# Masking the score tiles of the first six attention tiles on VectorE, and a new order of three GpSimd steps

## The chip, the cores and the metric

The kernel runs on one core of a Trainium2 chip, as one launch. The metric is the device time of that launch in microseconds (us), the median of several runs. The core's engines work side by side, each through a queue of its own: TensorE (PE in the profile; PEld are its weight loads), VectorE (DVE), ScalarE (ACT), GpSimd (POOL) and SyncE (SP), which here only issues DMA transfers. An engine takes its instructions strictly in the order in which they stand in its queue, and waits where an instruction needs something that another engine has not finished.

## What is computed

Three layers, one after the other, over 3072 tokens of width 384, all in float32. The first is a linear attention with a decaying state, 4 batches by 8 heads, 768 steps, head size 48:

```python
for t in range(S):
    kt, vt, rt, wt = (k[:, :, t], v[:, :, t], r[:, :, t], w[:, :, t])
    cur = np.einsum('bhd,bhe->bhde', u[None] * kt, vt)
    y[:, :, t] = np.einsum('bhd,bhde->bhe', rt, state + cur)
    state = wt[:, :, :, None] * state + np.einsum('bhd,bhe->bhde', kt, vt)
```

The second layer is an MLP, and the third a mixture of 8 experts of which each token takes the best one:

```python
h = x @ w_in;  g = np.maximum(h, 0.0) + alpha * np.minimum(h, 0.0);  x = g @ w_out
...
expert_idx = np.argmax(x @ w_gate, axis=1)
h = np.maximum(xe @ w1[e], 0.0);  ye = h @ w2[e];  out[mask] = gate_w[mask, None] * ye
```

## The kernel before

**Tiles and blocks.** The attention works in 24 tiles of 128 tokens, and three tiles make one of 8 blocks, on which the MLP then works (16 steps f of 128 hidden columns each). The attention of a block's tiles runs between the MLP steps of the block before. Block 0's MLP has a further job in it: `w_in` and `w_out` arrive as float32 and are split into a high and a low part, so that a product of float32 matrices can be made of three faster matmuls. The expert layer follows from about 560 us on.

**One attention tile**, with the names of the trace. `ex` (L291) is the running product of the decays; r is multiplied by it (L306, POOL) and k by its inverse `rec` (L315 to L331; L333, all DVE). PE then makes the scores, keys by queries, for eight heads in two PSUM tiles `pa` (L371). Only keys that lie before the query may count, so ACT copies each `pa` to `at` in SBUF (L379), and POOL sets the rest of `at` to zero (L383). The query's own key is dealt with apart: POOL multiplies r, k and u over the 48 elements of a head (`rk`, two steps, L338 and L339), DVE sums them to one number `c` per head (L344), and POOL multiplies v by it (`cv`, L351, two instructions). The state needs the transposed keys (`kt`, L401, ACT) and the decays over a whole tile (`pm`, L362, ACT), and is updated on DVE or POOL (L423 to L426). PE makes the output from `at`, `cv` and the state (L438 to L459), and DVE and ACT take it out of PSUM in a high and a low part (`xth`, `xtl`, L464, L469).

**MLP steps.** PE makes nine matmuls into `ph` (L611; there are two `ph` buffers), ACT takes the negative part `gn` (L614), DVE adds it to `ph` (`gt`, L616, which frees `ph`), and ACT and DVE split the result (`gh`, L622; `gl`, L624) for the nine matmuls of the second product (L637). When a block's sixteen steps are done, the three PSUM tiles `py` are copied to `x` (L648: the second on DVE, the others on ACT), and PE's next block needs their place. DVE then forms the gate's sums from `x` (L512).

**Weights.** Per piece of weights ACT copies the raw words (L216), DVE takes them apart in three integer steps (L220, L221, L224), ACT casts the high part (`wih`, `woh`, L237), and DVE subtracts to get the low one (`wil`, `wol`, L241).

**What sets the order.** `OPS` gives for each of a tile's steps a slot, counted from the tile's own start slot `s_tile(i)` in units of one MLP step; the prologue (tiles 0 to 2, and the start of tile 3) has a table of its own, `PRO_OPS`. In the prologue all engines run in the order of the slots. From then on PE and POOL do, while a scheduler sets the order of DVE, ACT and SP from its own model of costs; for the last part PE and DVE go by the slots. `constants()` builds small tables on POOL at slot 34, among them `tri`, a 128x128 triangle of ones. `rk` and `cv` have one buffer each, `ps_a`, the PSUM pool of `pa`, has three.

Of the kernel before, what the change touches and what calls it, by code (L numbers as in the profile page):

```python
# [11 lines left out]
BF16 = mybir.dt.bfloat16  # L12
# [3 lines left out]
ALU = mybir.AluOpType  # L16
# [10 lines left out]
NP = H // 2  # L27
# [39 lines left out]

NBACK = 7

DMW = 2 * 512 + NP * 129 + 1  # L70


OPS = {
# [3 lines left out]
}  # L77
# [30 lines left out]
def attention_mlp_moe(ctx, tc, dmaj, tmaj, ub, alpha, w_in, w_out, w_gate, w_gate_b, wexp, out):  # L108
    nc = tc.nc
    vec, act, pool, pe, sp = nc.vector, nc.scalar, nc.gpsimd, nc.tensor, nc.sync  # L110
# [3 lines left out]
    cst = ctx.enter_context(tc.tile_pool(name="cst", bufs=1))  # L114
# [17 lines left out]
    def load_tile(i):  # L132
        if i < NB:
            both = wp.tile([128, DMW + TMW], F32, tag="W", name="both")
            dm, tm = both[:PR, :DMW], both[:, DMW:]
            if i == 0:
# [4 lines left out]
        else:  # L141
            dm = ap.tile([PR, DMW], F32, tag="dm", name="dm")
            tm = ap.tile([128, TMW], F32, tag="tm", name="tm")
# [23 lines left out]
    pool.memset(inj, 0.0)  # L167
    ident = cst.tile([128, 128], F32, name="ident")
    make_identity(nc, ident)
    ub_s = cst.tile([128, DM], F32, name="ub_s")  # L170
    al_s = cst.tile([128, NF1], F32, name="al_s")
    oma_s = cst.tile([128, NF1], F32, name="oma_s")
# [69 lines left out]

        return rebase, words, high, low

    tri = cst.tile([128, 128], BF16, name="tri")
    iom = cst.tile([128, E], F32, name="iom")
    tokid = cst.tile([128, NTILE], I32, name="tokid")
    one16 = cst.tile([1, 2 * E], F32, name="one16")
# [11 lines left out]
        sp.dma_start(out=x2d[NT : NT + 1, :].rearrange("o (a t) -> o a t", a=KC), in_=apat[0:1, 0:KC, 1:129])  # L260

    def constants():
        pool.memset(tri, 1.0)
        pool.affine_select(
            out=tri, in_=tri, pattern=[[1, 128]], compare_op=ALU.is_gt, fill=0.0, base=0, channel_multiplier=-1
        )
        pool.iota(iom, pattern=[[1, E]], base=-E, channel_multiplier=0, allow_small_or_imprecise_dtypes=True)
        pool.iota(tokid, pattern=[[128, NTILE]], base=0, channel_multiplier=1)
        pool.memset(one16, 1.0)
        pool.iota(ebase, pattern=[[0, 2], [NT, E]], base=0, channel_multiplier=0, allow_small_or_imprecise_dtypes=True)  # L270
        pool.iota(iow, pattern=[[0, 2], [128, E]], base=0, channel_multiplier=0, allow_small_or_imprecise_dtypes=True)
        pool.iota(iou, pattern=[[1, NA + ULOOP], [0, 1]], base=0, channel_multiplier=0, allow_small_or_imprecise_dtypes=True)
        pool.iota(ioe, pattern=[[-1, NHALF], [0, 1]], base=-1, channel_multiplier=0, allow_small_or_imprecise_dtypes=True)
        pool.memset(acc_t[0], 0.0)
# [4 lines left out]
    def att_tile(i, s0):  # L279
        cx = {}  # L280
# [93 lines left out]
        def scores_out(jj):  # L374
            if i == 1:
                at = spare_t[0][:, 512 * jj : 512 * jj + 512].rearrange("p (a t) -> p a t", a=NP)
            else:
                at = ap.tile([128, NP, 128], F32, tag=f"at{jj}", name=f"at{jj}", bufs=1)
            act.copy(at, cx["pa"][jj])  # L379
            cx[jj] = at  # L380

        def mask(jj):
            pool.affine_select(  # L383
                out=cx[jj],
                in_=cx[jj],
                pattern=[[0, NP], [1, 128]],
                compare_op=ALU.is_gt,
                fill=0.0,
                base=0,
                channel_multiplier=-1,  # L390
            )
# [74 lines left out]
        def x_low():  # L466
# [5 lines left out]
            "scan": scan, "r": decay_r, "rec0": lambda: rec(0), "rec1": lambda: rec(1), "k": lambda: rec(2),  # L472
            "rk": diag, "c": diag_sum, "cv": diag_v, "sc": scores,
            "a0": lambda: scores_out(0), "m0": lambda: mask(0), "a1": lambda: scores_out(1), "m1": lambda: mask(1),
            "yst": yst, "yav0": lambda: yav(0), "yav1": lambda: yav(1), "xh": x_out, "xl": x_low,
        }
# [491 lines left out]
    at_slot(PT0 + 0.25, lambda: sp.dma_start(out=wg_s, in_=w_gate))  # L968
    at_slot(PT0 + PRO_FILL, fill)
    at_slot(GATE_CONST, constants)  # L970
    for i in range(1, NTILE):
        at_slot(s_tile(i - 2) + 7 if i > NB + 1 else PT0 + 0.1 * i, lambda i=i: load_tile(i))
# [17 lines left out]
    for i in range(NTILE):  # L990
        att_tile(i, s_tile(i))
# [54 lines left out]
    with tc.For_i(0, nrem, 1) as iv:  # L1046
        tb = qp.tile([1, 1, 2], I32, tag="tb", name="tb", bufs=1)
        sp.dma_start(
            out=tb, in_=tabd[:, ds(iv * 2, 2)].rearrange("p (o c) -> p o c", o=1)
# [80 lines left out]
```

## Time and profile before

| | us |
|---|---|
| median of 3 runs | 850.41 (849.59 to 852.24) |
| the profiled execution | 848.63 |
| its span in the trace | 846.8 |

| engine | busy, us | share of the span |
|---|---|---|
| PE | 800.0 | 94% |
| DVE | 611.5 | 72% |
| ACT | 383.1 | 45% |
| POOL | 306.6 | 36% |

Shares of the whole span are means over stages. The stages that matter are 12 to 122 us (prologue and block 0, with the splitting of the weights), 122 to 200 us (block 1), 200 to 560 us (blocks 2 to 7), and the expert layer after that. A duration in brackets at the end of a row of the trace is the time in which the engine stood idle before the instruction, and behind it stands who released it.

### The profile page before, as it was taken

To read this page: it belongs to the slowest core of one execution; us is meant where nothing else is said; L and a number is where in the kernel's file an instruction comes from. 1 tells how busy PE (TensorE), PEld (TensorE's weight loads), DVE (VectorE), ACT (ScalarE), POOL (GpSimd) and SP (SyncE) were. 2 spreads that over 40 slices of the span, in tenths; PEclk is the share of its full clock that TensorE was granted. 3 is DMA by queue.
4 is the path that set the end of the run, shared out by engine and by line. 5 is a ranking of instruction groups with operands and counts; after the bars stand their busy time and mean duration, and the time that the engine had idled before them with its cause. 6 is when DMAs were issued, how large, how long until landed. Compare 5 with 4: busy or idle time off the path is not lost. (4 is left out here: it accounts for less than half of the span.)

```text
span 846.8 us, 15713 instructions
## 1 busy us (share of the span) xinstructions
PE 800.0 (94%) x6032; PEld 752.2 (89%) x6032; DVE 611.5 (72%) x1145; ACT 383.1 (45%) x730; POOL 306.6 (36%) x326
## 2 busy tenths in 40 slices
PE   6777999999999999999999999999899999999994
PEld 4567788999899999899999989989899999999993
DVE  5999995458958968967977953556856676767761
ACT  2465554334334243243343333355446566665641
POOL 6845562343324334334333431130433233223301
PEclk9889999999999999999999999999999999999998
DMA  9825652223123122124123200066277677686820
GB/s 284 256 87 205 216 179 96 66 69 96 38 96 69 63 70 86 46 70 124 35 68 96 67 2 29 2 242 214 95 254 250 216 239 256 229 299 200 297 95 20
DMA packets 30516, 114.80 MB, mean 136 GB/s; under 512 B 8229, under 2 KB 11592, under 8 KB 30440
## 3 DMA queue, kind: packets, MB, share of 16 engines
q1 hardware_dynamic: 26088, 103.53, 37.7%
q0 software_dynamic: 4352, 10.26, 3.2%
q8 instruction: 48, 0.79, 0.4%
q14 instruction: 28, 0.23, 0.1%
HBM read 104.11 MB, written 10.45 MB: 135 GB/s over the span
## 5 line engine op out<-in xcount | busy, mean ns | idle before, releaser
L611 PE MATMUL ph<-xth,wih 128*128 128x384 f32 x384 | 135.7, 353 | 13.6 <-DVE gt L616 10.3
L637 PE MATMUL py<-woh,gh 128*128 128x384 f32 x384 | 134.8, 351 | 1.7 <-DVE x L648 1.7
L611 PE MATMUL ph<-xth,wil 128*128 128x384 f32 x384 | 130.5, 340 | 3.7 <-DVE wil L241 3.7
L611 PE MATMUL ph<-xtl,wih 128*128 128x384 f32 x384 | 129.7, 338 | 0.1
L637 PE MATMUL py<-woh,gl 128*128 128x384 f32 x384 | 129.1, 336 | 0.0
L637 PE MATMUL py<-wol,gh 128*128 128x384 f32 x384 | 128.9, 336 | 0.0
L622 ACT CAST gh<-gt 128x384 fp32r<-128x384 f32 x128 | 65.7, 513 | 138.6 <-DVE gt L616 137.8
L616 DVE SCALAR_TENSOR_TENSOR gt<-gn,oma_s,ph 128x384 f32<-128x384 f32 x128 | 77.8, 608 | 54.6 <-ACT gn L614 54.4
L624 DVE TENSOR_TENSOR gl<-gt,gh 128x384 fp32r<-128x384 f32 x128 | 85.8, 670 | 30.6 <-ACT gh L622 28.3
L614 ACT ACTIVATE gn<-ph 128x384 f32<-128x384 f32 x128 | 62.4, 488 | 83.3 <-PE ph L611 80.1
L842 DVE SCALAR_TENSOR_TENSOR gl<-ph,gh 128x256 fp32r<-128x256 f32 x96 | 40.4, 422 | 73.3 <-ACT gh L840 73.1
L611 PEld LDWEIGHTS ph<-xth,wih 128*128 128x128 f32 x384 | 72.8, 189 | 20.7 <-DVE gt L616 13.0
L383 POOL TENSOR_SCALAR_AFFINE_SELECT at<-at 128x512 f32<-128x512 f32 x46 | 39.8, 884 | 124.0 <-ACT at L379 124.0
L512 DVE SCALAR_TENSOR_TENSOR sink<-x,wgb 128x384 f32<-128x384 f32 x120 | 82.8, 713 | 1.5 <-ACT x L648 1.2
L911 POOL DMA_INDIRECT out<-ys,meta x28 | 28.2, 1009 | 150.7 <-ACT ys L908 93.3
L837 PE MATMUL ph<-xh,w1h 128*128 128x256 f32 x288 | 81.2, 282 | 1.7 <-DVE gl L842 1.6
L837 PE MATMUL ph<-xh,w1l 128*128 128x256 f32 x288 | 80.9, 281 | 0.0
L837 PE MATMUL ph<-xl,w1h 128*128 128x256 f32 x288 | 80.3, 279 | 0.0
L637 PEld LDWEIGHTS py<-woh,gh 128*128 128x128 f32 x384 | 72.4, 189 | 7.9 <-issue 2.8
L611 PEld LDWEIGHTS ph<-xth,wil 128*128 128x128 f32 x384 | 72.9, 190 | 5.2 <-DVE wil L241 5.2
L611 PEld LDWEIGHTS ph<-xtl,wih 128*128 128x128 f32 x384 | 72.9, 190 | 0.4 <-DVE xtl L469 0.4
L637 PEld LDWEIGHTS py<-woh,gl 128*128 128x128 f32 x384 | 72.4, 188 | 0.6 <-DVE gl L624 0.6
(218 smaller groups left out, 1864.2 us busy)
## 6 DMA issues: line engine op xcount, KB each, us to landing
raw<-w SPq DMA_DIRECT2D x64, 768.0 KB, 5.0
tm<-tmaj SPq DMA_DIRECT2D x21, 704.0 KB, 4.3
dm<-dmaj SPq DMA_DIRECT2D x21, 674.2 KB, 4.9
raw<-w_out SPq DMA_DIRECT2D x8, 768.0 KB, 4.3
raw<-w_in SPq DMA_DIRECT2D x7, 768.0 KB, 4.8
x2d<-x SPq DMA_DIRECT2D x8, 576.0 KB, 4.0
both<-tmaj SPq DMA_DIRECT2D x3, 704.0 KB, 9.5
wgb<-w_gate_b SPq DMA_DIRECT2D x2, 768.0 KB, 4.4
```

The source lines that it names most:

```text
L383: pool.affine_select(out=cx[jj], in_=cx[jj], pattern=[[0, NP], [1, 128]], compare_op=ALU.is_gt, fill=0.0, base=0, channel_multiplier=-1,)
L512: vec.scalar_tensor_tensor(out=sink, in0=x2[:, j, :], scalar=1.0, in1=wgb_t[h][:, e, :], op0=ALU.mult, op1=ALU.mult, accum_out=cx["l"][:, ...
L611: pe.matmul(ph, lhsT=w, rhs=x[:, c, :], start=k == 0, stop=k == 3 * KC - 1)
L614: act.activation(gn, ph, AF.Relu, scale=-1.0)
L616: vec.scalar_tensor_tensor(out=gt, in0=gn, scalar=oma_s[:, f : f + 1], in1=ph, op0=ALU.mult, op1=ALU.add)
L622: act.copy(gh, gt)
L624: vec.tensor_tensor(out=gl, in0=gt, in1=gh.bitcast(F32), op=ALU.subtract)
L637: pe.matmul(y_t[blk][j], lhsT=g[:, sl], rhs=w, start=f == 0 and m == 0, stop=f == NF1 - 1 and m == 2,)
L837: pe.matmul(ph, lhsT=w, rhs=x, start=k == 0, stop=k == 3 * KC - 1)
L842: vec.scalar_tensor_tensor(out=gl, in0=ph, scalar=0.0, in1=gh.bitcast(F32), op0=ALU.max, op1=ALU.subtract)
L911: pool.indirect_dma_start(out=out, out_offset=bass.IndirectOffsetOnAxis(ap=d["meta"][:, j, 0:1], axis=0), in_=ys, in_offset=None, bounds_c ...
```

## The change

For the tiles 0 to 5 (`NMASK = 6`) the copy of a score tile and its mask become one instruction: DVE multiplies `pa`, read out of PSUM, by `tri`, which is read once per head, and writes `at`. ACT's copies and POOL's masks of these six tiles fall away, 12 of each. So that `tri` is there in time, POOL builds it in the setup at the program's start and no longer in `constants()`. In `OPS` the slots of `r` and `rk` change places, so that from tile 4 on POOL does `rk`'s two steps first and `r`'s product after them (the first steps of tile 3 belong to the prologue, which has its own table). The diff:

```diff
+NMASK = 6
...
 OPS = {
-    "scan": -9, "r": -9, "rec0": -7, "rec1": -5, "k": -3, "rk": -6, "c": 0, "cv": 0, "sc": 0,
+    "scan": -9, "rk": -9, "rec0": -7, "rec1": -5, "k": -3, "r": -6, "c": 0, "cv": 0, "sc": 0,
...
     make_identity(nc, ident)
+    tri = cst.tile([128, 128], BF16, name="tri")
+    pool.memset(tri, 1.0)
+    pool.affine_select(
+        out=tri, in_=tri, pattern=[[1, 128]], compare_op=ALU.is_gt, fill=0.0, base=0, channel_multiplier=-1
+    )
...
-    tri = cst.tile([128, 128], BF16, name="tri")
...
     def constants():
-        pool.memset(tri, 1.0)
-        pool.affine_select(
-            out=tri, in_=tri, pattern=[[1, 128]], compare_op=ALU.is_gt, fill=0.0, base=0, channel_multiplier=-1
-        )
...
-            act.copy(at, cx["pa"][jj])
             cx[jj] = at
+            if i < NMASK:
+                keep = tri.rearrange("p (o t) -> p o t", o=1).to_broadcast([128, NP, 128])
+                vec.tensor_tensor(out=at, in0=cx["pa"][jj], in1=keep, op=ALU.mult)
+            else:
+                act.copy(at, cx["pa"][jj])
 
         def mask(jj):
+            if i < NMASK:
+                return
             pool.affine_select(
```

What stands where on the engines: PE's order does not change. POOL's queue around tile 4, before (the first rows are tile 3's `cv` and masks, the last three tile 4's):

```order
L351 TENSOR_TENSOR cv<-tm,c 128x256
L351 TENSOR_TENSOR cv<-tm,c 128x128
L383 AFFINE_SELECT at_531<-at_531 128x512
L383 AFFINE_SELECT at_534<-at_534 128x512
L306 TENSOR_TENSOR dm<-dm,ex 112x512
L338 TENSOR_TENSOR rk<-tm 128x384
L339 TENSOR_TENSOR rk<-rk,ub_s 128x384
```

and after, where the lines of the code stand two further down:

```order
L353 TENSOR_TENSOR cv<-tm,c 128x256
L353 TENSOR_TENSOR cv<-tm,c 128x128
L340 TENSOR_TENSOR rk<-tm 128x384
L341 TENSOR_TENSOR rk<-rk,ub_s 128x384
L308 TENSOR_TENSOR dm<-dm,ex 112x512
```

The masks are gone and `rk` stands right behind `cv`; the product with r (`dm`) is last.

DVE's queue around the first `gt` of block 0, before (the first row is the sum `c` of tile 3):

```order
L344 TENSOR_REDUCE c<-rk 128x8
L291 SCALAR_TENSOR_TENSOR ex<-dm,apat 112x516
L241 TENSOR_TENSOR wil_123<-v_455,wih_122 128x3x256
L220 TENSOR_SCALAR v_487<-v_487 128x768
L315 RECIPROCAL inj<-ex 112x4
L221 SCALAR_TENSOR_TENSOR v_487<-raw,v_487 128x768
L220 TENSOR_SCALAR v_529<-v_529 128x768
L224 SCALAR_TENSOR_TENSOR v_487<-raw,v_487 128x768
L616 SCALAR_TENSOR_TENSOR gt<-gn,oma_s,ph 128x384
```

and after (L346 is `c`, L227 to L231 the splitting, L384 the new mask, L624 `gt`, L632 `gl`):

```order
L346 TENSOR_REDUCE c<-rk 128x8
L293 SCALAR_TENSOR_TENSOR ex<-dm,apat 112x516
L248 TENSOR_TENSOR wil_125<-v_451,wih_124 128x3x256
L227 TENSOR_SCALAR v_483<-v_483 128x768
L317 RECIPROCAL inj<-ex 112x4
L346 TENSOR_REDUCE c<-rk 128x8
L228 SCALAR_TENSOR_TENSOR v_483<-raw,v_483 128x768
L624 SCALAR_TENSOR_TENSOR gt<-gn,oma_s,ph 128x384
L231 SCALAR_TENSOR_TENSOR v_483<-raw,v_483 128x768
L632 TENSOR_TENSOR gl<-gt,gh 128x384
L384 TENSOR_TENSOR at_527<-pa_500,tri 128x512
L384 TENSOR_TENSOR at_529<-pa_501,tri 128x512
```

Tile 4's `c` has come up from far behind to a place ahead of the first `gt`, and one step of the splitting has gone behind that `gt`.

DVE's queue where block 1 ends and its second `py` is copied, before:

```order
L616 SCALAR_TENSOR_TENSOR gt<-gn,oma_s,ph 128x384
L512 SCALAR_TENSOR_TENSOR sink,lg<-x_2103,wgb 128x384
L624 TENSOR_TENSOR gl<-gt,gh 128x384
L648 COPY x_2103<-py_1374 128x384
L512 SCALAR_TENSOR_TENSOR sink,lg<-x_2103,wgb 128x384 x3
```

and after (L656 is the copy of `py`, L520 the gate's sums):

```order
L624 SCALAR_TENSOR_TENSOR gt<-gn,oma_s,ph 128x384
L346 TENSOR_REDUCE c<-rk 128x8
L656 COPY x_2091<-py_1364 128x384
L632 TENSOR_TENSOR gl<-gt,gh 128x384
L520 SCALAR_TENSOR_TENSOR sink,lg<-x_2091,wgb 128x384 x4
```

The sum `c` of tile 10, which stood behind the gate's sums, now stands ahead of the copy. The same holds for tiles 13, 16, 19 and 22 and the copies of blocks 2 to 5.

## Rows read from the trace of the kernel before

**Rows 1.** Windows: from:to, us, busy us (instructions) of PE, PEld, DVE, ACT, POOL, PEclk, DMA, GB/s
```profile
12.00:122.00 110.00, 88.82 (x726) 75.66 (x726) 105.72 (x138) 55.55 (x104) 66.68 (x43) 0.92 0.63 208
...
200.00:560.00 360.00, 356.56 (x2752) 333.96 (x2752) 268.86 (x636) 130.80 (x295) 123.39 (x159) 1.00 0.22 66
```

**Rows 2.** Waits of PE, 38 to 140 us: us in total, times, longest us
```profile
PE ph L611 <- DVE gt L616: 6.0, 1, 6.0
PE ph L611 <- DVE wil L241: 3.7, 4, 2.0
...
```

**Rows 3.** Waits of PE, 200 to 560 us
```profile
PE ph L611 <- DVE gt L616: 3.4, 4, 1.1
```

**Rows 4.** Groups of DVE by form: busy us, mean ns of one, idle before
```profile
L469 DVE TENSOR_TENSOR xtl<-px,xth 128x384 fp32r<-128x384 f32 x24 | 13.1, 546 | 0.1
L885 DVE TENSOR_TENSOR glb<-pht,ghb 128x256 fp32r<-128x256 f32 x16 | 6.7, 421 | 6.2 <-ACT ghb L883 6.2
```

**Rows 5.** Waits of DVE, 12 to 122 us
```profile
DVE c L344 <- POOL rk L339: 1.7, 2, 0.9
DVE ex L291 <- DMA both<-dmaj: 1.1, 1, 1.1
...
DVE st L423 <- ACT pm L362: 0.5, 1, 0.5
DVE v L220 <- ACT v L216: 0.2, 1, 0.2
```

**Rows 6.** Timeline of POOL, 43 to 57 us: start us, us, instruction
```profile
43.83 2.99 POOL L351 TENSOR_TENSOR cv<-tm,c 128x256 f32<-128x256 f32 x2 [3.96 <-DVE c L344]
50.81 1.98 POOL L383 TENSOR_SCALAR_AFFINE_SELECT at<-at 128x512 f32<-128x512 f32 x2 [3.99 <-ACT at L379]
...
56.01 1.61 POOL L339 TENSOR_TENSOR rk<-rk,ub_s 128x384 f32<-128x384 f32 x1
```

**Rows 7.** Timeline of DVE, 46 to 58 us
```profile
46.48 0.17 DVE L315 RECIPROCAL inj<-ex 112x4 f32<-112x4 f32 x1
...
47.55 0.55 DVE L220 TENSOR_SCALAR v<-v 128x768 uint32<-128x768 uint32 x1
48.02 0.95 DVE L224 SCALAR_TENSOR_TENSOR v<-raw,v 128x768 uint32<-128x768 uint32 x1
48.89 0.60 DVE L616 SCALAR_TENSOR_TENSOR gt<-gn,oma_s,ph 128x384 f32<-128x384 f32 x1
...
52.18 1.42 DVE L224 SCALAR_TENSOR_TENSOR v<-raw,v 128x768 uint32<-128x768 uint32 x1
...
56.66 1.37 DVE L220 TENSOR_SCALAR v<-v 128x768 uint32<-128x768 uint32 x1
```

**Rows 8.** Timeline of POOL, 102 us: tile 5's masks
```profile
101.70 6.68 POOL L383 TENSOR_SCALAR_AFFINE_SELECT at<-at 128x512 f32<-128x512 f32 x2 [6.67 <-ACT at L379]
```

**Rows 9.** Tile `at`, its masks: duration ns least, median, most; first and last start
```profile
L383 POOL TENSOR_SCALAR_AFFINE_SELECT at<-at x46: 624/635/6098, 10.9 to 503.3; 128x512 f32<-128x512 f32 x46
```

**Rows 10.** Timelines of POOL, DVE and PE where block 0 ends, 127 to 132 us
```profile
127.87 1.19 POOL L306 TENSOR_TENSOR dm<-dm,ex 112x512 f32<-112x512 f32 x1
129.02 1.01 POOL L338 TENSOR_TENSOR rk<-tm 128x384 f32<-128x384 f32 x1
130.10 1.00 POOL L339 TENSOR_TENSOR rk<-rk,ub_s 128x384 f32<-128x384 f32 x1
...
131.13 0.55 DVE L344 TENSOR_REDUCE c<-rk 128x8 f32<-128x384 f32 x1 [3.21 <-POOL rk L339]
...
132.21 0.44 PE L637 MATMUL py<-woh,gh 128*128 128x384 f32 x1 [1.72 <-DVE x L648]
```

**Rows 11.** Timelines of DVE and PE where block 1 ends, 197 to 200 us
```profile
198.68 0.55 DVE L648 COPY x<-py 128x384 f32<-128x384 f32 x1
...
200.16 0.33 PE L637 MATMUL py<-woh,gh 128*128 128x384 f32 x1
```

**Rows 12.** Timeline of DVE in block 2: tile 10's `c`
```profile
226.54 0.55 DVE L344 TENSOR_REDUCE c<-rk 128x8 f32<-128x384 f32 x1 [1.07 <-POOL rk L339]
```

## The prediction
> **What bounds the kernel now.** I read the windows first [rows 1]. From 12 to 122 us DVE is busy for 105.72 of 110 us: it splits the weights there beside its share of the attention, and what is added to DVE or taken from it there moves the end of that stretch. PE has 88.82 us of work in it, and the waits of PE [rows 2] say whom it stands for: 6.0 us for block 0's first `gt`, 3.7 us in four waits for a low part `wil`, both DVE's. From 200 to 560 us it is the other way round: PE is busy for 356.56 of 360 us, DVE for 268.86 [rows 1]. All that is left to gain there is 3.4 us, four waits of PE for `gt` [rows 3]. The row behind them: DVE stands 1.07 us at tile 10's `c`, for POOL's `rk` [rows 12], and the `gt` behind that `c` comes late. The copies and masks that go belong to ACT, busy for 55.55 of 110 us, and to POOL, busy for 66.68; neither bounds the stretch by itself. So the change loads the engine that bounds the first stretch and frees two that don't; whether it pays depends on what POOL's work costs DVE, and on where DVE's waits go.
>
> **The change part by part.**
>
> *Twelve masks on DVE.* No instruction of before multiplies 128x512 out of PSUM by a broadcast. The nearest rows subtract 128x384 out of PSUM in 546 ns and 128x256 in 421 ns [rows 4], so about 1 ns for a further column, and 512 columns make 0.68 us (estimated from these two). DVE starts an instruction about 0.08 us before the end of the one before (48.02 + 0.95 against 48.89, [rows 7]), so each takes 0.60 us of the queue. Bounds: 0.47 us, as if the narrower form did, and 0.70. Tile 0's two fall into the 1.1 us in which DVE waits for tile 1's load [rows 5] and cost nothing; ten cost 6.0 us (4.7 to 7.0). ACT's twelve copies give nothing back by themselves, for ACT is not the bound. `tri` at the start: a quarter of a mask's width, at most a mask's 0.635 us [rows 9] on POOL; I take 0 and keep 0.6 for the range.
>
> *Tile 4's `c` ahead of the first `gt`.* In the new order of DVE this `c` stands behind the reciprocal that ends at 46.48 + 0.17 = 46.65 [rows 7], and in POOL's queue `rk`'s two steps stand behind tile 3's `cv`, which ends at 43.83 + 2.99 = 46.82 [rows 6]. Undisturbed they take 131.1 − 129.02 = 2.1 us [rows 10], so `c` can start at about 48.95, and DVE stands for 2.3 us. Queued behind it on DVE are a step of the splitting and the first `gt`, for which PE has already been waiting; from there all of block 0 is late. If `cv` runs as fast as it does where DVE leaves it alone, 0.6 us of this goes; if `rk` is stretched as in [rows 6], 0.6 us comes on top: 1.7 to 2.9. The `c` as such (0.55 us) is no extra work, since it goes from a later place.
>
> *Waits of DVE that go.* POOL has `rk` ready sooner: one of the two waits for it, 0.8 us; the waits for `pm` and for the rebased words (0.5 and 0.2 us) end since ACT has fewer copies [rows 5]. Together −1.5 us, between 0 and −2.
>
> *Work moved behind the last `wil`.* In the printed order a `gt`, a `gl` and a step of the splitting that stood ahead of block 0's last `wil` now stand behind it: about 0.53 + 0.47 + 0.47 us, −1.5 us for what PE waits for.
>
> *What POOL's masks cost DVE.* This is the term that decides. While POOL did tile 3's masks, r and `rk` (50.81 to 57.62, 6.8 us, [rows 6]), four DVE instructions with two inputs in SBUF or a 768-column step were stretched; the first took 1.42 us where its like takes 0.95, the last 1.37 against 0.55 [rows 7]; with the two between, 2.56 us in all. That is 0.38 us of DVE for each us of POOL. Tile 5's masks show the other side: they took 6.68 us instead of 1.27 [rows 8, 9], so there POOL stood back and DVE lost nothing. Ten masks and copies off POOL are 10 × 0.635 = 6.3 us undisturbed: between nothing and 6.3 us of DVE. At 0.38 that is 2.4 us; with 0.7 us for tile 4's `rk`, which now runs while DVE stands (0.38 × 2), I take −3.1 us.
>
> The Trainium skill, "Perfetto Trace Analysis", section "Optimizing Scalar/DVE Operations", says that where DVE is saturated some of its work may be offloaded to ScalarE, or even to GpSimd, and that between those two and DVE an offload to GpSimd might not help, since it shares a read port with DVE. By that the change goes the wrong way: nothing would come back, and the sum below would be the slower rival's. That DVE is saturated, its 105.72 of 110 us bear out; that nothing comes back, the stretched rows do not.
>
> *The sum for the first stretch*: 6.0 + 2.3 − 1.5 − 1.5 − 3.1 = +2.2 us at the last `wil` of block 0.
>
> *Where block 0 ends*, PE waits 1.72 us for the copy of `py`, because `c` of tile 7 stands ahead of it on DVE and waits 3.21 us for POOL [rows 10]. POOL does r (1.19 us) and then `rk` there; without r in front, `c` comes 129.02 − 127.87 = 1.15 us sooner, and PE with it, since the wait is longer than that. −1.2, so +1.0 us after block 0.
>
> *Blocks 2 to 7.* `c` of tiles 10, 13, 16, 19, 22 moves ahead of the copy of a block's second `py`, where `rk` is again free of r. DVE's wait of 1.07 us in front of the late `gt` [rows 12] goes from there. Does the new place cost anything? Before, that copy ends at 198.68 + 0.55 = 199.2, and PE needs it at 200.16 [rows 11]: a margin of about 0.9 us, into which a `c` of 0.47 us fits and a longer wait does not. I take 2.8 of the 3.4 us [rows 3] as gained (bounds 0 and 3.4).
>
> **Sum**: +1.0 − 2.8 = −1.8 us. The profiled execution took 848.63 us, so 846.8 by this sum; the median of the runs shown lies 1.8 us above it, at 850.41, and the forecast in its terms is 850.41 − 1.8 = 848.6 us. What a measurement of this kernel can tell from no change is about 0.3%, that is 2.55 us: 847.9 to 853.0.
>
> **The rivals.**
>
> *Slower: DVE simply has more to do.* If POOL's masks cost DVE nothing, as in [rows 8], the 3.1 us don't come back; and if DVE reaches its old waits no later, the 1.5 us stay too. Then the first stretch is 6.0 + 2.3 − 1.5 = +6.8, after block 0 it is +5.6, and with the 2.8 us of the later blocks the sum is +2.8 us: 853.2 us, and 854.6 if half of those fail as well. It is measurably slower from the point at which less than 0.3 of these 4.6 us come back. For it: DVE's saturation; against it: the stretched rows. 0.20.
>
> *Faster: each mask on POOL costs DVE its whole length.* Then 6.3 + 0.7 = 7.0 us come back instead of 3.1, the first stretch is −1.7, block 0 ends at −2.9, and the later waits go altogether: −6.3 us, 844.1, at the end of it. Halfway between this and the forecast's price, with 5.05 us back, block 0 at −0.95 and 3.2 us later, it is −4.1 us: 846.3, the value of this rival. It is measurably faster from 3.9 us given back on. For it: single instructions were stretched by up to 0.8 us in the rows that stand there; against it: the average of 0.38. 0.28. The Trainium skill, "SBUF — State Buffer", section "Who interferes with whom", says that a DVE instruction with two SBUF inputs contends with one of GpSimd that reads SBUF, and, of the two-port modes, that the one that comes first holds the shared port pair for its whole instruction while the other fully blocks; read for all of these instructions, this rule gives the far end, 844.1. The row of tile 5's masks agrees that the one of the two can stand back for long, but there it was POOL [rows 8].
>
> *The same: the wait only moves with `c`.* In the later blocks `c` waits ahead of the copy for `rk` by as much as before (1.07 us), and the margin of 0.9 us, less its own 0.47, covers 0.43 of it. PE then stands 0.64 us at each of the five copies, 3.2 us against the 3.4 of now, and the 2.8 us aren't gained: +1.0 us, 851.4. For it: in POOL's queue there is other work of the tile ahead of `rk`; against it: r, 1.19 us, no longer is. 0.12.
>
> **How the numbers follow.** Forecast 0.40, of which 0.08 fall below the bound of 0.3%; faster rival 0.28, all below it; the same 0.12; slower rival 0.20, which I count as slower whole, since its value lies at the bound and its reach above it. Faster 0.36, same 0.44, slower 0.20. The range goes from the far end of the faster rival, 844.1, to that of the slower one, 854.6: single runs of before lie 1.8 us above their median, so I cut neither end.
>
> **What the new trace should show.** The DVE masks at 0.6 to 0.7 us; a wait of about 2.3 us at the second `c` behind 46 us, and PE's wait for the first `gt` ending near 50.7 us instead of 49.5; PE at block 0's last `wil` some 2 us later than before; `c` at the end of block 0 waiting some 2 us instead of 3.21; no wait of 1.07 us in block 2 and PE's waits there mostly gone, with no new wait for a copy of `py`. The forecast is wrong above all if the DVE instructions beside `cv` and `rk` are stretched as before without the masks, if the wait at tile 4's `c` is far from 2.3 us, or if PE meets a wait that isn't there now, such as one for scores' PSUM tiles that DVE frees late, or for weights whose loads SP issues in another order.

## The result: the kernel takes longer

| | us |
|---|---|
| before, median of 5 runs | 850.41 (849.06 to 852.24) |
| after, median of 5 runs | 857.48 (855.51 to 860.52) |
| ratio after to before | 1.0078, 95% interval 1.0057 to 1.0100 |
| profiled execution after | 860.52, span 858.8 |

So the change costs 6.6 us (4.8 to 8.5), where 848.6 was forecast and 854.6 was the upper end of the range. The profiled execution is the longest of its five, and the profiled one of before, at 848.63 us, is shorter than all five of before: their differences are read for where time goes, and sizes are taken from the ratios. Part of the surplus is there before the change can act. The first `c`, which waits for tile 0's load, starts at 12.53 us in this trace and at 10.94 in the one before; it lies between 10.0 and 12.8 in the traces of the experiments, whichever kernel runs.

Most of the 12.0 us between the two traces lies in the prologue and block 0. That block's last copy of `py` ends at 132.2 us before and at 141.2 after. From there to the same copy of block 1 the traces take 67.1 and 67.4 us, on to block 7's 381.0 and 382.1, and to the end 266.6 and 268.1.

The windows of the changed kernel (from:to, us, busy us of PE, PEld, DVE, ACT, POOL, then granted clock, DMA share, GB/s), to be read beside [rows 1]:

```profile
12.00:122.00 110.00, 87.77 (x676) 73.59 (x674) 99.03 (x135) 47.10 (x88) 36.91 (x32) 0.86 0.59 186
...
200.00:560.00 360.00, 355.71 (x2753) 331.58 (x2752) 266.97 (x644) 132.27 (x300) 121.74 (x159) 1.00 0.21 62
```

POOL is relieved as meant, from 66.68 to 36.91 us. But DVE, which had 4.3 us without work between 12 and 122 us, now has 11.0, though twelve instructions were given to it: it stands and waits. (The window is cut at fixed times, and the changed kernel has done less of its work by 122 us.) PE runs at a lower granted clock there, 0.86 instead of 0.92. In the later window PE is no busier than before.

What PE waits for, 38 to 140 us and then 200 to 560 us, beside [rows 2] and [rows 3]:

```profile
PE ph L619 <- DVE gt L624: 7.1, 1, 7.1
PE ph L619 <- ACT wih L244: 5.0, 3, 2.1
PE ph L619 <- DVE wil L248: 2.7, 5, 1.0
PE ph L619 <- DVE xtl L477: 1.6, 1, 1.6
```

```profile
PE ph L619 <- DVE gt L624: 3.8, 5, 1.0
PE py L645 <- DVE x L656: 0.4, 1, 0.4
```

The first `gt` is late, and none of the 3.4 us in the later blocks is gone. What DVE waits for, 12 to 122 us, beside [rows 5]:

```profile
DVE c L346 <- POOL rk L341: 8.3, 3, 4.6
DVE v L227 <- ACT v L223: 3.7, 4, 1.9
DVE gl L632 <- ACT gh L630: 1.0, 2, 0.7
```

Of the 8.3 us, 4.6 belong to tile 0's `c`, mostly ahead of this window. The row to look at is the next largest, in the timeline of DVE (start us, us, instruction, idle before it):

```profile
46.39 0.55 DVE L346 TENSOR_REDUCE c<-rk 128x8 f32<-128x384 f32 x1
...
49.31 0.17 DVE L317 RECIPROCAL inj<-ex 112x4 f32<-112x4 f32 x1
52.29 0.55 DVE L346 TENSOR_REDUCE c<-rk 128x8 f32<-128x384 f32 x1 [2.80 <-POOL rk L341]
52.76 1.44 DVE L228 SCALAR_TENSOR_TENSOR v<-raw,v 128x768 uint32<-128x768 uint32 x1
54.12 0.60 DVE L624 SCALAR_TENSOR_TENSOR gt<-gn,oma_s,ph 128x384 f32<-128x384 f32 x1
```

The second of the two `c` is tile 4's. DVE stands 2.80 us for it, and the first `gt`, for which PE waits, is queued behind it.

### The profile page after: what moved, and what is told of

It reads as the page before. It is cut to its first block, busy times and chain, and to the rows that moved or that the text cites. A ratio compares the mean times of both kernels' runs of the same rounds, so it can differ in the third digit from the quotient of the medians.

```text
span 858.8 us, 15674 instructions
## 1 busy us (share of the span) xinstructions
PE 810.6 (94%) x6032; PEld 760.0 (88%) x6032; DVE 611.9 (71%) x1157; ACT 376.8 (44%) x718; POOL 270.2 (31%) x314
## 5 line engine op out<-in xcount | busy, mean ns | idle before, releaser
L624 DVE SCALAR_TENSOR_TENSOR gt<-gn,oma_s,ph 128x384 f32<-128x384 f32 x128 | 77.8, 608 | 52.2 <-ACT gn L622 52.0
L632 DVE TENSOR_TENSOR gl<-gt,gh 128x384 fp32r<-128x384 f32 x128 | 86.3, 674 | 32.7 <-ACT gh L630 30.4
L520 DVE SCALAR_TENSOR_TENSOR sink<-x,wgb 128x384 f32<-128x384 f32 x120 | 75.9, 668 | 0.1
L645 PEld LDWEIGHTS py<-wol,gh 128*128 128x128 f32 x384 | 73.1, 190 | 0.0
```

What stands on the lines that cost most here:

```text
L520: vec.scalar_tensor_tensor(out=sink, in0=x2[:, j, :], scalar=1.0, in1=wgb_t[h][:, e, :], op0=ALU.mult, op1=ALU.mult, accum_out=cx["l"][:, ...
L624: vec.scalar_tensor_tensor(out=gt, in0=gn, scalar=oma_s[:, f : f + 1], in1=ph, op0=ALU.mult, op1=ALU.add)
L632: vec.tensor_tensor(out=gl, in0=gt, in1=gh.bitcast(F32), op=ALU.subtract)
L645: pe.matmul(y_t[blk][j], lhsT=g[:, sl], rhs=w, start=f == 0 and m == 0, stop=f == NF1 - 1 and m == 2,)
```

## Experiments

Each kernel ran in five rounds beside the kernel before. "us" is the ratio's distance from 1 times 850.4 us, with its 95% interval. Two theories stood at the start: that the masks of tiles 0 to 2 delay the prologue, and that tile 4's `c` ahead of the first `gt` (the c-first theory) makes the loss. An experiment that moves one step changes more than that step: from the new order of POOL or the new masks the scheduler writes DVE's, ACT's and in part SP's order anew. Only e11 and e12 leave the other engines' orders as they were.

### Which part: the order, or which tiles' masks

The new GpSimd order alone:

```diff
-NMASK = 6
+NMASK = 0
```

> The new order of GpSimd alone (rk ahead of r from tile 4 on); all masks stay on GpSimd, with ScalarE's copies. In VectorE's printed order the sum c of tile 4 keeps its old place behind the sixth gt; only the c of tiles 9, 10, 13, 15, 16, 19, 21, 22 move. Theory of the prediction: 1.2 us at the end of block 0 and 2.8 us in blocks 2 to 7 come back, so -4.0 us, 846.4. Rival, read from the trace of the changed kernel (PE's waits for gt after 280 us are still 3.8 us): only the 1.2 us at the end of block 0 or less come back, -1.2 to 0 us, and PE meets waits for gt in the later blocks as before (about 3.4 us).

Measured: 0.9995 (0.9974 to 1.0017), −0.4 us (−2.2 to +1.4). PE's waits, 38 to 140 us and 200 to 560 us:

```profile
PE ph L619 <- DVE gt L624: 5.1, 1, 5.1
PE ph L619 <- DVE wil L248: 4.1, 4, 2.1
PE ph L619 <- ACT wih L244: 3.9, 3, 2.5
```

```profile
PE ph L619 <- DVE gt L624: 3.2, 5, 0.8
```

The wait for the copy of `py` where block 0 ends is gone (1.72 us before, [rows 10]), and the waits of the later blocks are there as before. The order brings nothing that can be measured, and it isn't the loss.

The masks alone, and then by tiles, with GpSimd's old order:

```diff
-    "scan": -9, "rk": -9, ..., "r": -6,
+    "scan": -9, "r": -9, ..., "rk": -6,
...
+NMASK = 6                        (e2)
+NMASK = 3                        (e3)
+            if NB <= i < NMASK:  (e4)
```

> The masks of tiles 0 to 5 on VectorE alone; GpSimd keeps r ahead of rk. In VectorE's printed order c of tile 4 again stands ahead of the first gt, so it is the masks and not the new GpSimd order that bring it there. Theory: the whole loss belongs to the masks, and since r (1.2 us) now stands ahead of rk, the wait at tile 4's c is about 4.0 instead of 2.8 us: +8 us, 858 to 859. Rival: the loss comes from the two parts together; then this is at +2 to +4 us.

> Masks on VectorE for tiles 0, 1 and 2 only, GpSimd's order as before. c of tile 4 keeps its old place. Theory 1 (the prologue's fixed VectorE order lets the masks delay everything behind them, and PE falls to half clock): +3 us of the loss is here, 853.5; the c of tile 3 comes about 3 us later than 43.1 us, as in the changed kernel (46.4). Theory 2 (the loss is the c ahead of the first gt): within 1 us of before.

> Masks on VectorE for tiles 3, 4 and 5 only, GpSimd's order as before. c of tile 4 stands ahead of the first gt. Theory 2 (the loss is the c ahead of the first gt, and what follows on weight loads): +4 to +5 us, 854.5 to 855.5, with a wait of 3 to 4 us at this c. Theory 1 (the loss is the prologue's): within 1 us of before.

Measured: e2 1.0069 (1.0040 to 1.0099), +5.9 us (3.4 to 8.4); e3 0.9999 (0.9981 to 1.0017), −0.1 us (−1.6 to +1.4); e4 1.0071 (1.0046 to 1.0096), +6.0 us (3.9 to 8.2). The prologue theory falls: its six masks cost nothing that these runs can tell, and the masks of tiles 3 to 5 carry the loss. In the printed orders it is these that bring tile 4's `c` ahead of the first `gt`; with the new POOL order and the old masks (e1) it stays where it was.

### Tile 3 against tiles 4 and 5

```diff
-NMASK = 6
+NMASK = (3,)       (e5; in e6 it is (4, 5))
...
-            if i < NMASK:
+            if i in NMASK:
```

> Only tile 3's two masks on VectorE, GpSimd's order as before. In VectorE's printed order this alone brings tile 4's c ahead of the first gt. Theory c-first (the loss is the wait at this c, ahead of the gt that PE stands for): +5 to +7 us, as with the masks of tiles 3 to 5 together, though VectorE has only 1.2 us more to do. Rival, more work (each mask of block 0 costs VectorE 0.6 us and what is behind it): a third of the loss, about +2 us.

> The masks of tiles 4 and 5 on VectorE, GpSimd's order as before. Tile 4's c keeps its old place; tile 5's c goes from behind the eighth gt to behind the twelfth. Theory c-first: within 1.5 us of before. Rival, more work: two thirds of the loss, about +4.5 us.

Measured: e5 1.0076 (1.0057 to 1.0095), +6.5 us (4.9 to 8.1); e6 1.0029 (1.0010 to 1.0047), +2.5 us (0.9 to 4.0). Two masks cost more than the four others. In e5 r again stands ahead of `rk` on POOL, and the wait at tile 4's `c` is longer by 1.1 us, about the length of r:

```profile
52.21 0.55 DVE L346 TENSOR_REDUCE c<-rk 128x8 f32<-128x384 f32 x1 [3.94 <-POOL rk L341]
```

But e6 is above what the c-first theory allowed it (1.5 us). Its four masks take 0.60 us of DVE's queue each: 2.4 us, so the measured 2.5 us fit their full price. Tile 5's `c` has moved back too, so the masks are not quite alone in it.

### The place of tile 4's `c` by itself

The kernel before, with one of POOL's steps moved and no work added to DVE; its order, ACT's and SP's are written anew from that:

```diff
-                at_slot(s0 + OPS[n], fn)
+                at_slot(s0 + (-11 if (i, n) == (NB + 1, "rk") else OPS[n]), fn)
```

> The kernel before with one thing moved: GpSimd does tile 4's rk right behind tile 3's cv, so that VectorE's printed order has tile 4's c ahead of the first gt; all masks stay on GpSimd, and VectorE has no work added. Theory c-first: PE's first gt comes 2 to 3 us later and the kernel takes +3 to +6 us. Rival, more work: within 1 us of before.

Measured: 1.0050 (1.0030 to 1.0070), +4.3 us (2.6 to 6.0). The timeline of DVE shows the wait of the changed kernel again:

```profile
48.65 0.55 DVE L344 TENSOR_REDUCE c<-rk 128x8 f32<-128x384 f32 x1 [2.80 <-POOL rk L339]
...
50.46 0.61 DVE L616 SCALAR_TENSOR_TENSOR gt<-gn,oma_s,ph 128x384 f32<-128x384 f32 x1
```

But this does not price the wait. The same trace has a second one, at tile 6's `c`, that neither the kernel before nor the changed one has, and PE stands for a high part that comes late behind it:

```profile
109.22 0.55 DVE L344 TENSOR_REDUCE c<-rk 128x8 f32<-128x384 f32 x1 [3.66 <-POOL rk L339]
...
116.14 0.55 PE L611 MATMUL ph<-xth,wih 128*128 128x384 f32 x1 [4.54 <-ACT wih L237]
```

Ahead of it the first wait was made good. Counted from tile 3's `c`, the first `gt` starts after 7.70 us (5.76 before), but the twelfth after 58.3 us (58.6 before). So in this trace the loss is the second wait's, and what the wait at tile 4's `c` costs by itself is not shown. The opposite, the whole change with this `c` held behind:

```diff
         def mask(jj):
-            if i < NMASK:
+            if i < NMASK and i != NB:
                 return
```

> The whole change, and GpSimd masks tile 3's at a second time (the result is the same), so that tile 4's rk must wait for VectorE's masks, and tile 4's c stands behind the seventh gt in VectorE's printed order. Theory c-first: most of the loss goes, at most +2 us. Rival, more work: the loss stays, +5 to +7 us. A third theory, that the order in which SP issues the loads of weights (a tile's load now ahead of a piece of w_out) makes the loss, also has it stay, since that order is here as in the changed kernel.

Measured: 1.0049 (1.0033 to 1.0066), +4.2 us (2.8 to 5.6). That is 2.4 us less than the whole change, with intervals that overlap: it is not most of the loss, and neither the c-first theory nor its rival holds alone. The traces, one of each kernel, add something. Counted from tile 3's `c`, the twelfth `gt` starts after 60.0 us in e8 (masks of tile 3 on DVE, no wait at tile 4's `c`), after 58.3 in e7 (the wait, no masks), and after 64.3 to 65.2 in the four kernels that have both (e2, e4, e5 and the whole change); before it is 58.6. So the two together put block 0 back there by about 6 us, more than the one and the other by themselves. At block 1's first `gt` it is 81.1 us before, 85.4 in e8 and 87.4 with the whole change.

One way in which they can do so stands in the trace of the changed kernel. SP issues a load of `w_out` at 67.58 us (61.43 before), having waited for DVE's third step of an earlier piece; ACT stands 2.22 us for it, until 74.25, and then DVE stands 1.89 us for the words that ACT rebases, where it stood 0.2 before [rows 5]:

```profile
74.25 0.89 ACT L223 ACTIVATE v<-raw 128x768 f32<-128x768 f32 x1 [2.22 <-DMA raw<-w_out]
...
75.18 0.56 DVE L227 TENSOR_SCALAR v<-v 128x768 uint32<-128x768 uint32 x1 [1.89 <-ACT v L223]
```

The load of a tile that SP now issues ahead of this one does not hold it up: behind that load SP stands another 2.5 us for DVE. What is left in e8 was put to a third theory of this kind, that tile 3's masks delay the loads of weights:

```diff
-                at_slot(s0 + OPS[n], fn)
+                at_slot(s0 + OPS[n] + (1 if i == NB and n in ("a0", "a1", "m0", "m1") else 0), fn)
```

> As the whole change with GpSimd's second mask of tile 3 (e8_hold), but tile 3's score masks one slot later, which puts them in VectorE's printed order behind the third step of the second piece of weights instead of ahead of it; tile 4's c stays behind the seventh gt. Theory ring (what is left in e8_hold, +4.2 us, comes because tile 3's masks stand ahead of the steps that free the weights' load buffer, so that the next load is issued 2.4 us later): the load of w_in follows that of w_out by about 5 us as in the kernel before, not 7, and the time is within 2 us of before. Rival, more work (VectorE simply has ten masks more): as e8_hold, +4 us.

Measured: 1.0065 (1.0042 to 1.0089), +5.5 us (3.6 to 7.6). The load of `w_in` did come sooner, 3.6 us behind that of `w_out` instead of 7.0 in e8, but the next load of `w_out` followed 10.1 us after it instead of 5.7, and no time was won; the twelfth `gt` starts 61.8 us after tile 3's `c`. The theory of the loads falls in this form: the masks stand ahead of one piece of weights or of the next, and DVE has them to do either way. That late loads are part of what the masks and the wait cost together is not excluded by it.

The whole change with tile 3's masks left out of it:

```diff
         def scores_out(jj):
...
-            if i < NMASK:
+            if i < NMASK and i != NB:
...
         def mask(jj):
-            if i < NMASK:
+            if i < NMASK and i != NB:
```

> The whole change except that tile 3's masks stay on GpSimd, with ScalarE's copies: ten masks on VectorE, the new GpSimd order, tile 4's c behind the sixth gt. If tile 3's two masks are what costs, by the place of tile 4's c and by the place of the weights' steps, this is at +0 to +3 us, as with the masks of tiles 4 and 5 alone (+2.5 us). If all masks cost alike, it is at +5.5 us, five sixths of the loss.

Measured: 1.0028 (1.0012 to 1.0043), +2.4 us (1.0 to 3.7), the same as the masks of tiles 4 and 5 alone. Leaving tile 3's two masks where they were takes back 4 of the 6.6 us; the kernel is still slower than before.

### What POOL's work costs DVE

The term on which the prediction turned, taken by itself in two kernels in which nothing else moves on any engine. In the first, ten masks are left out altogether:

```diff
         def mask(jj):
+            if i in (0, 1, 2, 4, 5):
+                return
             pool.affine_select(
```

> The kernel before without GpSimd's masks of tiles 0, 1, 2, 4 and 5 (they are left out and done nowhere, so part of the computation is missing; ScalarE's copies stay). Every other instruction stands where it stood on every engine, so this prices what GpSimd's ten masks cost by themselves, the term that decided in the prediction. Theory of the prediction: 0.38 us of VectorE for each of their 6.3 us come back, -2.4 us. Rival, they cost VectorE their whole length: -6.3 us. Rival, nothing comes back: within 1 us of before.

Measured: 1.0017 (0.9996 to 1.0037), +1.4 us (−0.3 to +3.1). This time is not the price of the masks alone. With part of the computation missing the tokens are routed by other numbers, and where the last block ends this trace has a wait of PE that is as long in no other:

```profile
561.53 0.44 PE L639 MATMUL py<-woh,gh 128*128 128x384 f32 x1 [2.33 <-ACT gh L624]
```

ACT stands ahead of it for a load of expert weights. SP issues that load behind one of `meta`, which waits until POOL's writes of the routing table `metad` have landed: before the second of the last three such writes POOL waits 4.34 us for the first to land here, and 2.56 to 3.28 in the thirteen other traces. That the wrong numbers make it so is likely, not shown. Until block 6 ends e11's trace is 1.7 us ahead of the one before (523.7 against 525.4), 0.9 of it by an earlier start. From the first `c` to block 1's first `gt`, the stretch in question, it takes 112.5 us instead of 113.3: 0.8 us come back, where 2.4 were forecast, by one trace of each. Its window from 12 to 122 us:

```profile
12.00:122.00 110.00, 90.64 (x738) 77.67 (x737) 106.29 (x140) 56.05 (x106) 51.12 (x33) 0.92 0.62 207
```

POOL has 15.6 us less than in [rows 1], and DVE is as busy as before. In the second, POOL gets work where it stood idle beside a busy DVE:

```diff
             pool.tensor_tensor(out=rk, in0=rk, in1=ub_s, op=ALU.mult)
+            if i == NB + 1:
+                for _ in range(16):
+                    pool.affine_select(
+                        out=rk, in_=rk, pattern=[[0, 3], [1, 128]], compare_op=ALU.is_gt, fill=0.0,
+                        base=1000, channel_multiplier=-1,
+                    )
```

> The kernel before with GpSimd work added where GpSimd stands idle and VectorE is busy: 16 selects of 128x384 that keep every value, in place on tile 4's rk, behind its two products (57.6 us) and ahead of the wait for tile 4's c (72.7 us). No other instruction moves on any engine. They are about 7.6 us of GpSimd, by the 635 ns of a 512-column mask. Theory of the prediction: 0.38 us of VectorE for each, +2.9 us. Rival, whole length: +7.6 us. Rival, nothing: within 1 us, and GpSimd's selects are the ones that get long.

Measured: 1.0048 (1.0032 to 1.0064), +4.1 us (2.7 to 5.4): between the two prices of the expectation, 0.54 us for each of the 7.6. The timelines of POOL and of DVE:

```profile
59.37 17.54 POOL L342 TENSOR_SCALAR_AFFINE_SELECT rk<-rk 128x384 f32<-128x384 f32 x16
```

```profile
71.08 0.89 DVE L220 TENSOR_SCALAR v<-v 128x768 uint32<-128x768 uint32 x1
71.89 1.26 DVE L241 TENSOR_TENSOR wil<-v,wih 128x768 fp32r<-128x768 f32 x1
73.08 0.87 DVE L630 TENSOR_TENSOR gl<-gt,gh 128x384 fp32r<-128x384 f32 x1
73.86 1.27 DVE L221 SCALAR_TENSOR_TENSOR v<-raw,v 128x768 uint32<-128x768 uint32 x1
75.06 0.60 DVE L622 SCALAR_TENSOR_TENSOR gt<-gn,oma_s,ph 128x384 f32<-128x384 f32 x1
75.58 0.95 DVE L224 SCALAR_TENSOR_TENSOR v<-raw,v 128x768 uint32<-128x768 uint32 x1
```

Undisturbed, the first four take 0.55, 0.95, 0.55 and 0.95 us: each is longer by 0.31 to 0.34. `gt`, with an operand in PSUM, keeps its 0.60. The last row is of the fourth's kind and keeps its 0.95: now the one engine gives way, now the other. The two kernels together: selects beside a busy DVE do cost it time, but taking away those that the kernel had gives little back.

## Why the prediction was wrong

**The bound was right, and the two costs where they arise.** DVE's work and waits between 12 and 122 us set the time, as the windows said. The masks take 681 ns each (0.68 was estimated), and two in a row 1.28 us, so 0.60 and 0.68 us of the queue. The wait at tile 4's `c` is 2.80 us where 2.3 was worked out, because `cv` took 3.15 us in place of 2.99 and the reciprocal came in sooner ahead of it; PE's wait for the first `gt` grew from 6.0 to 7.1 us, and this `gt` starts 7.0 us behind the start of tile 3's `cv` (54.12 − 47.08, the latter from POOL's timeline) where it was 5.1 (48.89 − 43.83, [rows 6, 7]). That block 0 as a whole is late by the wait, no more and no less, was assumed: e7 and e8 do not bear it out.

**The masks' sum was taken over the wrong tiles.** Four of the ten masks that I priced belong to tiles 1 and 2, and those cost nothing measurable (e3, −1.6 to +1.4 us); six masks of block 0 remain, 3.6 us, of which four measured 2.5 us (e6, 0.9 to 4.0).

**Of the five gains, one shows in the traces and none in the time.** These are the terms that failed, but for the fourth:
- *−3.1 for POOL's masks.* This is the largest of the five and was called the deciding term. A rate was taken from one stretch of 6.8 us in which POOL made masks, r and `rk`, and applied to masks wherever they stood. Where ten masks are left out, some 0.8 us come back instead of 2.4 (e11 up to block 1, by one trace), though work of the same kind in another place does cost (e12). Adding up, for all DVE instructions up to block 1's first `gt`, what each took beyond the shortest of its form in any of the traces, one gets 19.7 us before, 19.0 in e11 and 25.6 with sixteen selects. With masks moved and no wait at tile 4's `c` it is 18.2 to 19.2 (e8, e9, e10) and 22.1 (e6): no steady gain. The changed kernel has 15.1, less than forecast to remain, so there the term came, but at the price of waits: DVE stands for 11.0 us of the stretch instead of 4.3, and while it stands nothing of it is stretched.
- *−1.5 for DVE's old waits.* Those for `rk` (0.8) and `pm` (0.5) went, but the one for the rebased words grew from 0.2 to 3.7 us, and 1.0 for `gh` came.
- *−1.5 for work moved behind the last `wil`.* The printed order counts instructions, not waits; the last `wil` came 10.0 us later (121.54 against 111.53), 1.6 of them by the later start, not 2.2.
- *−1.2 where block 0 ends.* PE's wait for the copy of `py` did go, in the traces of all five kernels with POOL's new order, and `c` of tile 7 waits 1.49 us in the changed one instead of 3.21 [rows 10]; the time gained is within e1's interval, so it is neither shown nor excluded.
- *−2.8 in blocks 2 to 7.* A wrong reading. The `c` that waits 1.07 us at 226.54 us [rows 12] is not tile 10's, as I put it, but tile 11's: tile 10's starts at 207.03. The change doesn't lift tile 11's `c` out of the gate's work. After, it is

```profile
234.62 0.56 DVE L346 TENSOR_REDUCE c<-rk 128x8 f32<-128x384 f32 x1 [0.99 <-POOL rk L341]
```

and on POOL `rk` stands there without r in front, but behind tile 10's masks, which wait for ACT's copies:

```profile
230.49 1.72 POOL L391 TENSOR_SCALAR_AFFINE_SELECT at<-at 128x512 f32<-128x512 f32 x2 [12.23 <-ACT at L386]
232.18 1.31 POOL L340 TENSOR_TENSOR rk<-tm 128x384 f32<-128x384 f32 x1
233.57 1.02 POOL L341 TENSOR_TENSOR rk<-rk,ub_s 128x384 f32<-128x384 f32 x1
```

PE's waits for `gt` in these blocks are 3.8 us in five instead of 3.4 in four.

What is left of the sum is 3.6 us for six masks and 2.8 for the wait: 6.4, against 6.6 measured (4.8 to 8.5). That it comes so close is in part luck, since the sum's last term is not shown by itself. Shown, each with its interval, is that the masks of tiles 4 and 5 cost about their own 2.4 us (e6, e10), and that tile 3's two masks, with the new order that comes of them, bring the rest, about 4 (the change against e10; in e5, where r stands ahead of `rk` again, they cost 6.5). That these 4 are 1.2 for the masks and 2.8 for the wait is worked out, and the traces speak for more than a sum: at the twelfth `gt` the wait alone puts nothing back (e7), the masks without it 1.4 and 3.2 us (e8, e9), both together about 6. In e8, where the `c` is held, the time lies 1.8 us above e10; tile 3's masks can be 1.2 of them, and its second pair on POOL, at e12's 0.54, some 0.7 (estimated).

**The rivals.** The outcome is that of the slower one, DVE simply has more to do, with its condition nearly met (little comes back) and the later blocks' 2.8 us failing as well; it was priced up to 854.6, because it was allowed to keep at least half of the later gain. Its chance of 0.20 was too low. The third, that waits only move, has the outcome of blocks 2 to 7 but not its cause: PE stands 0.4 us at the copies of `py`, not 3.2, and 3.8 us for `gt`, much as before. Of the Trainium skill's two places, "Perfetto Trace Analysis", section "Optimizing Scalar/DVE Operations", gave the right side: with DVE saturated, work was moved to it from engines that were not. "SBUF — State Buffer", section "Who interferes with whom", agrees with e12 for the instructions with two inputs in SBUF and for `gt`, but the whole-length price made of it for POOL's masks does not show in e11, where 0.8 of 6.3 us come back.

**Open** is how tile 3's masks and the wait at tile 4's `c` cost more together than apart, with the loads of weights as a suspect; why the six masks of the prologue cost nothing, though in e3's trace tile 3's `c` starts at 44.6 us instead of 43.1; and what the lower granted clock takes. After, PE has 0.86 in the first stretch instead of 0.92, and 0.88 in e1, at the time of before, and in e10. After the wait for the first `gt` it is at about half, the lower of its two levels, in both kernels (0.50 from 47.4 to 54.2 us before, 0.51 from 52.6 to 59.5 after), so it comes with such waits; no run here takes it apart.

## What to carry to other kernels

A collision's price measured in one place is not what removing its cause gives back: leave the work out, with everything else in place, and time the stretch in question before counting on it, for a kernel that computes other numbers can lose time elsewhere. Where a scheduler sets an engine's order, look in the new order for what has come ahead of the instruction that the bound engine waits for; here one instruction of 0.55 us that was to be ready early made DVE stand 2.8 us. And when an experiment puts one wait in, read its whole trace for others before taking its time as the price of that wait. And follow a wait to the instance that waits, by counting tiles, before putting it down to an edit.

## What was not expected of the hardware

In e12 sixteen GpSimd selects of 384 columns took 17.5 us beside a busy VectorE, 1.1 us from one to the next, where the shortest took 0.52 us and 512-column masks take 0.64 undisturbed: both engines lose, and VectorE's integer step with one tensor input (L220, 0.89 us in place of 0.55) was stretched as much as those with two.
